# New loads and a computed order for the first 28 slices of a fused attention and gated-FFN kernel

## The chip, the cores and the metric

One core of a Trainium2 chip. The metric is the device time of one execution in microseconds (us). Spans in traces (first to last instruction) are some 2 us shorter than the device times of the same runs.

## The reference, cut to what matters

```python
# x: (B=8, H=8, S=512, D=64), state: (8, 8, 32, 64); all fp32
scores = scale * x @ state^T ; a = softmax(scores) ; xread = a @ state           # 512 rows per batch
scores2 = scale * state @ x^T ; a2 = softmax(scores2) ; sread = a2 @ x           # 32 rows per batch
y = concat([xread, sread], rows).transpose(0, 2, 1, 3).reshape(B * 544, 512)
out = (relu(y @ w_gate) * (y @ w_val)) @ w_out          # d_ff = 1536
```

The kernel folds the state into the gate and value weights (`U = state @ w`), so a batch's gate and value are `U^T @ a^T`. A batch has 12 gate/value slices of 128 columns of d_ff (`gv`), and 12 output pieces (`o`), each of four 512-column matmuls.

## The kernel before

Loads, in the order of issue:

```python
state_dma(nc.sync, 0, 2)                  # state of batches 0 and 1, fp32, hardware queue
x_dma_cast(0, 2)                          # batch 0 of x, cast to bf16 on load, by gpsimd's queue
make_identity(nc, id128)
nc.gpsimd.memset(xa[:, :, :, D:D + 1], 1.0)
for i in range(6):
    for s, d in ws:                       # ws = gate weights, value weights: cast on load
        w_dma(s, d, 256 * i, 256 * i + 256)
    if i == 1:
        x_dma_cast(1)                     # batch 1 behind two weight pairs
x_dma_cast(2); state_dma(nc.gpsimd, 2, B); wo_dma(0, 6); wo_dma(6, NF); x_dma(3, (nc.gpsimd,))
```

The head, up to the 28th gate/value slice, is a written order; what runs before the first slice is called the prelude below. Each engine does its own words from left to right. `spin` is a matmul on zeros for the clock, `xT`/`xo` a transpose of x and its copy out of PSUM, `sc`/`ex`/`nr`/`nx` scores, exp, row sum with reciprocal, scaling, `aT`/`ao` the transpose of the weights of attention and its copy, `c`/`co` (and `u`/`uo`) a fold (state times weights) and its eviction, the copy out of PSUM, to U, `ga`+`gb` one slice, `re` its ReLU on ACT, `mu` its product on VectorE (DVE), `o` an output piece, `sr` the state-read:

```text
spin.7 spin.1 stc.0.2.dve stT.0.2 sto.0.2.0.dve sto.0.2.1.dve xT.0.0 xT.0.1 xo.0.1.dve xo.0.0.act xT.0.3
xo.0.3.dve sc.0.0 xT.0.2 xo.0.2.dve ex.0.0 sc.0.1 nr.0.0 ex.0.1 c.0.0 nx.0.0 ...      # first slice soon after
... (cut)
```

After it a loop does one slice, one output piece and what is hung on that slice:

```python
for b in range(B):
    s, jf = {0: (2, 2), 1: (2, 3), 2: (2, 7), 3: (2, 11)}.get(b, (b - 1, 9))
    if b > 1:
        at(s, jf, sr, b)                  # state-read of batch b at slice jf of round s
```

PSUM: six banks in rotation for everything but the output (`ps_r`), two for the output.

The softmax here doesn't subtract the row's maximum and nothing guards it: scores larger than these inputs give would overflow.

Of the kernel before, what the change touches and what calls it, by code (L numbers as in the profile page):

```python
# [16 lines left out]
def kernel(  # L17
# [35 lines left out]
    ps_r = pool("ps_r", 6, PS)  # L53
    ps_o = pool("ps_o", 1, PS)
# [25 lines left out]
    def bank(name, o=None):  # L80

        if o is None:
            return ps_r.tile([128, 512], FP32, name=name, tag="r")
        return ps_o.tile([128, 512], FP32, name=name, tag=f"o{o}")
# [57 lines left out]
    def x_conv(b, half, eng):  # L142
        if half == 0:
            xb_alloc(b)
            xb[b] = xb[b].rearrange("p (c h d) -> p c h d", c=NC, h=H)
        hs = slice(HK * half, HK * half + HK)
        copy[eng](out=xb[b][:, :, hs].rearrange("p c h d -> p h c d"), in_=xf[b][:, hs])  # L147
# [9 lines left out]
    def x_T(b, j):  # L157

        if j == 0:
            xT_alloc(b)  # L160
        ps = bank("xT_ps").bitcast(BF16)[:, 0:512].rearrange("p (c t) -> p c t", c=NC)
        for c in range(NC):
            if b in cast_on_load:
                for h2 in range(2):
                    nc.tensor.transpose(ps[64 * h2:64 * h2 + 64, c], xb[b][:, c, 2 * j + h2], id128)  # L165
            else:
                nc.tensor.transpose(ps[:, c], xb[b][:, c, 2 * j:2 * j + 2].rearrange("p h d -> p (h d)"), id128)
        held["xT", b, j] = ps
# [5 lines left out]
    def att_sc(b, jp):  # L174
        if jp == 0:
            e_sn[b] = att.tile([128, 2, NC, NJ * Ns], BF16, name="e_sn", tag="e_sn", bufs=4)
            a_sn[b] = att.tile([128, 2, NC, NJ * Ns], BF16, name="a_sn", tag="a_sn")
        t = held["sc", b, jp] = bank("sc_ps")
        ps = t.rearrange("p (r c j n) -> p r c j n", r=2, c=NC, j=2)
        for c in range(NC):  # L180
            for jj in range(2):
                nc.tensor.matmul(ps[:, :, c, jj], xT[b][:, c, 2 * jp + jj], stT[:, b, 2 * jp + jj],  # L182
                                 start=True, stop=True)
# [15 lines left out]
    def att_scale(b, jp):  # L199
        e_v = by_pair(e_sn[b], jp).rearrange("p r (j n) -> p r j n", n=Ns)  # L200
        nc.vector.tensor_tensor(out=by_pair(a_sn[b], jp).rearrange("p r (j n) -> p r j n", n=Ns), in0=e_v,  # L201
                                in1=held["rc", b, jp].to_broadcast([128, 2 * NC, 2, Ns]), op=ALU.mult)
# [9 lines left out]
    def att_T(b, kc):  # L212
        if kc == 0:
            ans_alloc(b)
# [74 lines left out]
    def gv(b, jf, kcs=(0, 1)):  # L289
        if jf == 0 and kcs[0] == 0:  # L290
            hsb[b] = hpool.tile([128, NF, S], BF16, name="h_sb", tag="h_sb")
        if kcs[0] == 0:
            held["gv", b, jf] = [bank("gv_ps"), bank("gv_ps")], hsb[b][:, jf], S
        for w in range(2):
            for kc in kcs:
# [21 lines left out]
    o_n = [0]  # L317

    def o_bank():
        o_n[0] += 1  # L320
        return bank("o_ps", o_n[0] % 2)
# [11 lines left out]
    def fin_x(b, tsub):  # L333
        o_sb = opool.tile([128, d_model], FP32, name="o_sb", tag="o_sb")
        nc.scalar.copy(out=o_sb, in_=held["o", b, tsub])  # L335
# [36 lines left out]
    state_dma(nc.sync, 0, 2)  # L372
    x_dma_cast(0, 2)
# [4 lines left out]
    for i in range(6):  # L378
        for s, d in ws:
            w_dma(s, d, 256 * i, 256 * i + 256)  # L380
        if i == 1:
            x_dma_cast(1)
# [11 lines left out]
    warm_ps = bank("warm_ps", 0)  # L394

    def spin(n):
        for i in range(n):
            nc.tensor.matmul(warm_ps, warm[:, 0:128], warm, start=True, stop=True)
# [80 lines left out]
    for b in range(B):  # L479
        s, jf = {0: (2, 2), 1: (2, 3), 2: (2, 7), 3: (2, 11)}.get(b, (b - 1, 9))  # L480
# [48 lines left out]
```

## Time and profile before

| | before |
|---|---|
| device time, median of 3 | 231.95 us |
| span in the trace | 228.9 us |
| TensorE busy | 219.0 us, 96% |
| first gate/value slice | 14.21 us |
| first output slice | 36.29 us |
| slice 28, start of the loop | 59.21 us |

To read it: an engine at 96% can gain only where it is not busy or where it does nothing useful. The stages are cut at the first of a new kind of work, because the share of a whole span hides which stage is limited by what. The lines are in the prediction.

### The profile page before, as it was taken

The numbers are of one execution on the slowest core, as the hardware profiler recorded it, in microseconds if no ns is written. First come the engines' busy times: TensorE is split into PE (matmuls) and PEld (weight loads), VectorE is DVE, ScalarE is ACT, GpSimd is POOL, SyncE is SP. The second block draws the span as 40 slices with busy tenths as digits, with TensorE's granted clock in tenths as the row PEclk, the third lists the DMA queues.
The fourth block names the chain that finished last, engine by engine and source line by source line (L and its number), as shares of the span: only waits on it lengthen the run. The fifth ranks groups of instructions, "written<-read, shape, count | busy, mean of one in ns | idle before, by whom it ended". The sixth has DMA issues, their size and how long they took to land.

```text
span 228.9 us, 4751 instructions
## 1 busy us (share of the span) xinstructions
PE 219.0 (96%) x1916; PEld 105.1 (46%) x1916; DVE 133.5 (58%) x237; ACT 121.1 (53%) x233; POOL 43.1 (19%) x46
## 2 busy tenths in 40 slices
PE   7589899999998999999999999999999999999994
PEld 3345445454443444344444454444443444666543
DVE  3669878984669646764676568556765344222100
ACT  2469776664775645565555555554655444332221
POOL 8926252341052060006000510000000000000000
PEclk9769999999999999999999999999999999999999
DMA  7999999071715911393139413911311111111132
GB/s 100 174 195 196 214 217 272 21 137 49 223 54 112 279 63 54 79 222 115 53 90 224 146 46 92 140 46 46 94 46 49 46 47 47 49 47 64 73 95 92
DMA packets 36950, 25.21 MB, mean 110 GB/s; under 512 B 17248, under 2 KB 32352, under 8 KB 36928
## 3 DMA queue, kind: packets, MB, share of 16 engines
q1 hardware_dynamic: 25168, 16.78, 27.3%
q0 software_dynamic: 11424, 7.73, 21.5%
q10 hardware_dynamic: 336, 0.39, 0.7%
q8 instruction: 15, 0.25, 0.4%
q14 instruction: 7, 0.06, 0.1%
HBM read 18.35 MB, written 8.91 MB: 119 GB/s over the span
## 4 chain that ended last, share of the span: by engine, by line
PE 85%; DMA 9%; DVE 2%; POOL 1%; issue 1%; ACT 1%; POOLq 0%
PE o_ps L327 37%; PE gv_ps L286 34%; DMA wv_sb<-in_moe_w_val_dram 6%; PE gv_ps L304 5%; PE up L261 4%; DMA wg_sb<-in_moe_w_gate_dram 3%; PE sc_ps L182 1%; PE sr_ps L234 1%; DMA out_dram<-o_sb 1%; DVE a_sn L201 1%; PE upc L261 1%; POOL xb L112 1%; PE xT_ps L165 0%; PE srT_ps L247 0%; PE stT_ps L132 0%
## 5 line engine op out<-in xcount | busy, mean ns | idle before, releaser
L286 PE MATMUL gv_ps<-ans,U 128*128 128x512 bf16 x384 | 97.1, 381 | 1.1 <-DVE U L271 1.0
L327 PE MATMUL o_ps<-wo_sb,h_sb 128*128 128x512 bf16 x372 | 94.8, 379 | 0.0
L315 DVE TENSOR_TENSOR h_sb<-gv_ps,g_sb 128x512 bf16<-128x512 f32 x96 | 64.7, 688 | 42.6 <-ACT g_sb L311 38.3
L311 ACT ACTIVATE g_sb<-gv_ps 128x512 bf16<-128x512 f32 (+1 forms) x108 | 62.1, 578 | 45.7 <-PE gv_ps L286 34.8
L286 PEld LDWEIGHTS <-U 128*128 128x128 bf16 x384 | 35.3, 98 | 42.8 <-issue 5.7
L327 PEld LDWEIGHTS <-h_sb 128*128 128x128 bf16 x372 | 36.0, 98 | 41.1 <-issue 0.9
L335 ACT COPY o_sb<-o_ps 128x512 f32<-128x512 f32 x31 | 18.1, 585 | 21.5 <-PE o_ps L327 21.5
L271 DVE CAST U<-up 128x512 bf16<-128x512 f32 x35 | 22.5, 685 | 6.1 <-PE up L261 6.1
L271 ACT CAST U<-up 128x512 bf16<-128x512 f32 x37 | 19.9, 594 | 10.5 <-PE up L261 10.4
L147 POOL CAST xb<-xf 128x1024 bf16<-128x1024 f32 x10 | 10.6, 1089 | 68.9 <-DMA xf<-in_x_dram 48.8
L195 DVE TENSOR_REDUCE cs<-e_sn 128x16 f32<-128x512 bf16 x16 | 10.9, 683 | 9.2 <-ACT e_sn L189 9.2
L226 POOL COPY xa<-xb 128x2048 bf16<-128x2048 bf16 x8 | 15.0, 1896 | 5.7 <-issue 4.2
L315 DVE TENSOR_TENSOR hs_sb<-gv_ps,g_sb 128x256 bf16<-128x256 f32 x12 | 5.1, 425 | 15.3 <-PE gv_ps L304 10.5
L189 ACT ACTIVATE e_sn<-sc_ps 128x512 bf16<-128x512 f32 x16 | 9.6, 601 | 7.4 <-PE sc_ps L182 7.4
L201 DVE TENSOR_TENSOR a_sn<-e_sn,rc 128x512 bf16<-128x512 bf16 x16 | 12.4, 775 | 0.5
L261 PEld LDWEIGHTS <-stT 64*32 64x32 bf16 x480 | 5.3, 92 | 11.2 <-issue 10.3
L281 ACT CAST U<-upc 128x512 bf16<-128x512 f32 x14 | 7.6, 592 | 3.5 <-PE upc L261 3.4
L182 PEld LDWEIGHTS <-xT 128*128 128x128 bf16 x128 | 5.8, 100 | 4.0 <-DVE xT L171 0.7
L261 PE MATMUL up<-wg_sb,stT 64*32 64x512 bf16 x144 | 7.4, 386 | 0.0
L182 PE MATMUL sc_ps<-stT,xT 128*128 128x64 bf16 x128 | 6.7, 196 | 0.5 <-DVE xT L171 0.5
L304 PE MATMUL gv_ps<-br,wg_sb 128*128 128x256 bf16 x48 | 7.2, 273 | 0.0
L304 PE MATMUL gv_ps<-br,wv_sb 128*128 128x256 bf16 x48 | 7.2, 273 | 0.0
(54 smaller groups left out, 115.1 us busy)
## 6 DMA issues: line engine op xcount, KB each, us to landing
out_dram<-o_sb SPq DMA_DIRECT2D x31, 256.0 KB, 2.4
xf<-in_x_dram SPq DMA_DIRECT2D x4, 1024.0 KB, 6.0
wg_sb<-in_moe_w_gate_dram POOLq DMA_DIRECT2D x6, 256.0 KB, 11.3
wv_sb<-in_moe_w_val_dram POOLq DMA_DIRECT2D x6, 256.0 KB, 10.8
wo_sb<-in_moe_w_out_dram POOLq DMA_DIRECT2D x2, 768.0 KB, 15.1
xb<-in_x_dram POOLq DMA_DIRECT2D x2, 512.0 KB, 11.1
xf<-in_x_dram POOLq DMA_DIRECT2D x1, 1024.0 KB, 18.8
xb<-in_x_dram POOLq DMA_DIRECT2D x2, 256.0 KB, 4.7
```

What stands on the lines that cost most here:

```text
L182: nc.tensor.matmul(ps[:, :, c, jj], xT[b][:, c, 2 * jp + jj], stT[:, b, 2 * jp + jj], start=True, stop=True)
L195: nc.vector.reduce_sum(out=cs, in_=e_v, axis=AX.X)
L201: nc.vector.tensor_tensor(out=by_pair(a_sn[b], jp).rearrange("p r (j n) -> p r j n", n=Ns), in0=e_v, in1=held["rc", b, jp].to_broadcast([1 ...
L226: nc.gpsimd.tensor_copy(out=v.rearrange("p c h d -> p h c d"), in_=xb[b].rearrange("p c h d -> p h c d"))
L261: nc.tensor.matmul(dst[parity][32 * j:32 * j + 32], stT[r:r + 64, b, j, 32 * parity:32 * parity + 32], wsb[r:r + 64, j, lo:lo + n], start= ...
L271: copy[eng](out=U[b][:, w, kc, lo:lo + 512], in_=held["u", b, w, lo][kc])
L286: nc.tensor.matmul(ps[w], U[b][:, w, kc, f0:f0 + 128], ANS[b][:, kc].rearrange("p c t -> p (c t)"), start=(kc == 0), stop=(kc == NK - 1))
L304: nc.tensor.matmul(ps[w][:, 0:nt], wsb[:, j, f0:f0 + 128], br[:, j].rearrange("p b n -> p (b n)"), start=(j == 0), stop=(j == NJ - 1))
L311: nc.scalar.activation(out=g_sb[:, 0:n], in_=ps[0][:, 0:n], func=AF.Relu)
L315: nc.vector.tensor_tensor(out=dst, in0=ps[1][:, 0:n], in1=held["g", b, jf][:, 0:n], op=ALU.mult)
L327: nc.tensor.matmul(held["o", b, tsub], src[:, jf, tsub * 128:(tsub + 1) * 128], wo_sb[:, jf], start=(jf == 0), stop=(jf == NF - 1))
L335: nc.scalar.copy(out=o_sb, in_=held["o", b, tsub])
```

## The change

Intent: load batch 0 faster as plain fp32 on both hardware queues, have batch 1 early enough to do its attention before the first slice, keep the clock up with short spins in the waits, and take the order of the head and its PSUM banks from a computed schedule.

```diff
-    state_dma(nc.sync, 0, 2)
-    x_dma_cast(0, 2)
+    xf[0] = xin.tile([128, H, NC, D], FP32, name="xf", tag="xf")
+    for half in range(2):
+        for eng, h in ((nc.sync, HK * half), (nc.scalar, HK * half + 2)):
+            eng.dma_start(out=xf[0][:, h:h + 2], in_=x[0, h:h + 2].rearrange("h (p c) d -> p h c d", c=NC))
+        if half == 0:
+            state_dma(nc.sync, 0, 2)
+    x_dma_cast(1, 2)
...
-        if i == 1:
-            x_dma_cast(1)
...
+    given, turn = [], {"r": 0, "o": 0}      # bank(): the banks that a word names with @, else in turn
...
-    spin.7 spin.1 stc.0.2.dve stT.0.2 sto.0.2.0.dve sto.0.2.1.dve xT.0.0 xT.0.1 ...
+    stc.0.2.dve spin.4 spin.3.128 stT.0.2@0 sto.0.2.0.act xc.0.0.dve sto.0.2.1.act spin.8.128 xT.0.1@1 xT.0.0@2
+    xo.0.1.dve xo.0.0.act xc.0.1.dve spin.14.128 sc.0.0@3 xT.0.3@4 ex.0.0 xT.0.2@5 xo.0.3.act nr.0.0 xo.0.2.act
+    spin.22.128 sc.0.1@0 nx.0.0 xT.1.0@1 ... spin.11.128 gv.0.1@12 ...      (the rest of the head is cut)
...
-        s, jf = {0: (2, 2), 1: (2, 3), 2: (2, 7), 3: (2, 11)}.get(b, (b - 1, 9))
+        s, jf = {0: (2, 2), 1: (2, 3), 2: (2, 8), 3: (2, 11)}.get(b, (b - 1, 9))
```

`xc` is VectorE's conversion of half of batch 0. The last line: the state-read of batch 2 moves one slice later.

More of the change, by code (lines that the diff above doesn't have):

```diff
@@ L52 @@
     PS = bass.MemoryType.PSUM
-    ps_r = pool("ps_r", 6, PS)
-    ps_o = pool("ps_o", 1, PS)
+    psum = pool("psum", 1, PS)
     NK = 2
@@ L78, with bank @@
     copy = {"act": nc.scalar.copy, "dve": nc.vector.tensor_copy, "pool": nc.gpsimd.tensor_copy}
-    def bank(name, o=None):
-        if o is None:
-            return ps_r.tile([128, 512], FP32, name=name, tag="r")
-        return ps_o.tile([128, 512], FP32, name=name, tag=f"o{o}")
+    given, turn = [], {"r": 0, "o": 0}
+    def bank(name, kind="r"):
+        if given:
+            n = given.pop(0)
+        else:
+            n = turn["r"] % 6 if kind == "r" else 6 + turn["o"] % 2
+            turn[kind] += 1
+        return psum.tile([128, 512], FP32, name=name, tag=f"b{n}")
     held = {}
@@ L142, in x_conv @@
     def x_conv(b, half, eng):
-        if half == 0:
+        if b not in xb:
             xb_alloc(b)
@@ L157, in x_T @@
     def x_T(b, j):
-        if j == 0:
+        if b not in xT:
             xT_alloc(b)
@@ L174, in att_sc @@
     def att_sc(b, jp):
-        if jp == 0:
+        if b not in e_sn:
             e_sn[b] = att.tile([128, 2, NC, NJ * Ns], BF16, name="e_sn", tag="e_sn", bufs=4)
@@ L197, in att_sum, with att_scale @@
         nc.vector.reciprocal(out=rc, in_=cs)
-    def att_scale(b, jp):
+    def att_scale(b, jp, eng="dve"):
         e_v = by_pair(e_sn[b], jp).rearrange("p r (j n) -> p r j n", n=Ns)
-        nc.vector.tensor_tensor(out=by_pair(a_sn[b], jp).rearrange("p r (j n) -> p r j n", n=Ns), in0=e_v,
+        {"dve": nc.vector, "pool": nc.gpsimd}[eng].tensor_tensor(out=by_pair(a_sn[b], jp).rearrange("p r (j n) -> p r j n", n=Ns), in0=e_v,
                                 in1=held["rc", b, jp].to_broadcast([128, 2 * NC, 2, Ns]), op=ALU.mult)
@@ L212, in att_T @@
     def att_T(b, kc):
-        if kc == 0:
+        if b not in ANS:
             ans_alloc(b)
@@ L287, in gv_mm, with gv @@
                          start=(kc == 0), stop=(kc == NK - 1))
-    def gv(b, jf, kcs=(0, 1)):
-        if jf == 0 and kcs[0] == 0:
+    def gv(b, jf):
+        if b not in hsb:
             hsb[b] = hpool.tile([128, NF, S], BF16, name="h_sb", tag="h_sb")
-        if kcs[0] == 0:
-            held["gv", b, jf] = [bank("gv_ps"), bank("gv_ps")], hsb[b][:, jf], S
+        held["gv", b, jf] = [bank("gv_ps"), bank("gv_ps")], hsb[b][:, jf], S
         for w in range(2):
-            for kc in kcs:
+            for kc in range(NK):
                 gv_mm(held["gv", b, jf][0], b, jf, w, kc)
@@ L315, in mult @@
         nc.vector.tensor_tensor(out=dst, in0=ps[1][:, 0:n], in1=held["g", b, jf][:, 0:n], op=ALU.mult)
-    o_n = [0]
     def o_bank():
-        o_n[0] += 1
-        return bank("o_ps", o_n[0] % 2)
+        return bank("o_ps", "o")
     def out_mms(src, b, tsub, jfs):
@@ L331, in out_rows, with fin_x @@
         return out[b * SP: b * SP + S].rearrange("(p q) m -> q p m", q=NC)[tsub]
-    def fin_x(b, tsub):
+    def fin_x(b, tsub, eng="act"):
         o_sb = opool.tile([128, d_model], FP32, name="o_sb", tag="o_sb")
-        nc.scalar.copy(out=o_sb, in_=held["o", b, tsub])
+        copy[eng](out=o_sb, in_=held["o", b, tsub])
         nc.sync.dma_start(out=out_rows(b, tsub), in_=o_sb)
@@ L392, in x_next, with spin @@
         x_trans_dma(b)
-    warm_ps = bank("warm_ps", 0)
-    def spin(n):
+    warm_ps = psum.tile([128, 512], FP32, name="warm_ps", tag="b7")
+    def spin(n, cols=512):
         for i in range(n):
-            nc.tensor.matmul(warm_ps, warm[:, 0:128], warm, start=True, stop=True)
-    steps = {"spin": spin, "stc": state_conv, "stT": state_T, "sto": state_out, "xT": x_T, "xo": x_out,
+            nc.tensor.matmul(warm_ps[:, 0:cols], warm[:, 0:128], warm[:, 0:cols], start=True, stop=True)
+    steps = {"spin": spin, "stc": state_conv, "stT": state_T, "sto": state_out, "xc": x_conv, "xT": x_T, "xo": x_out,
@@ L403 @@
              "sc": att_sc, "ex": att_exp, "nr": att_sum, "nx": att_scale, "aT": att_T, "ao": att_out,
-             "c": c_unit, "co": c_out, "u": u_unit, "uo": u_out, "ga": lambda b, jf: gv(b, jf, (0,)),
-             "gb": lambda b, jf: gv(b, jf, (1,)), "re": relu, "mu": mult, "o": out_part,
-             "of": lambda b, t, eng: fin_x(b, t), "xn": x_next, "xp": x_pad, "sr": lambda b: (sr_mm(b), sr_norm(b))}
+             "c": c_unit, "co": c_out, "u": u_unit, "uo": u_out, "gv": gv, "re": relu, "mu": mult, "o": out_part,
@@ L407 @@
+             "of": fin_x, "xn": x_next, "xp": x_pad, "sr": sr_mm, "sn": sr_norm}
     program = """
-    spin.7 spin.1 stc.0.2.dve stT.0.2 sto.0.2.0.dve sto.0.2.1.dve xT.0.0 xT.0.1 xo.0.1.dve xo.0.0.act xT.0.3
-    xo.0.3.dve sc.0.0 xT.0.2 xo.0.2.dve ex.0.0 sc.0.1 nr.0.0 ex.0.1 c.0.0 nx.0.0 co.0.0.0.act co.0.0.1.act
-    nr.0.1 c.1.0 co.1.0.0.act nx.0.1 aT.0.0 aT.0.1 ao.0.0.act c.0.1 co.1.0.1.dve c.1.1 ao.0.1.dve co.0.1.1.dve ga.0.0
-    gb.0.0 co.0.1.0.act co.1.1.1.dve ga.0.2 co.1.1.0.act gb.0.2 re.0.0 re.0.2 ga.0.3 gb.0.3 mu.0.0 ga.0.1 mu.0.2
@@ L412 @@
-    re.0.3 gb.0.1 re.0.1 xT.1.0 xT.1.1 xo.1.0.act mu.0.3 xT.1.2 xo.1.2.act xT.1.3 mu.0.1 xo.1.1.dve stc.2.8.pool xp.0 xp.1
-    xo.1.3.dve c.0.2 co.0.2.0.act sc.1.0 co.0.2.1.dve c.1.2 co.1.2.0.dve sc.1.1 ex.1.0 co.1.2.1.act ga.0.5 gb.0.5
-    nr.1.0 ex.1.1 re.0.5 ga.0.4 gb.0.4 c.0.3 nx.1.0 re.0.4 mu.0.5 co.0.3.0.act co.0.3.1.act mu.0.4 c.1.3
-    co.1.3.1.act c.0.4 nr.1.1 co.0.4.0.dve co.1.3.0.act ga.0.6 gb.0.6 ga.0.7 gb.0.7 co.0.4.1.act nx.1.1
-    re.0.6 ga.0.9 re.0.7 gb.0.9 aT.1.0 aT.1.1 mu.0.6 ao.1.0.act ga.0.8 mu.0.7 re.0.9 ao.1.1.dve gb.0.8 ga.1.0 gb.1.0 re.0.8 mu.0.9
@@ L417 @@
-    ga.1.1 re.1.0 gb.1.1 mu.0.8 mu.1.0 ga.1.6 re.1.1 mu.1.1 gb.1.6 ga.1.3 gb.1.3 ga.1.2 re.1.6 gb.1.2 re.1.3 mu.1.6
-    re.1.2 mu.1.3 stT.2.4 ga.1.5 gb.1.5 ga.1.7 mu.1.2 sto.2.4.1.act sto.2.4.0.act re.1.5 gb.1.7 ga.1.4 gb.1.4
-    re.1.7 mu.1.5 re.1.4 o.0.0 c.0.5 xT.2.0 co.0.5.0.act mu.1.7 mu.1.4 xT.2.1 xT.2.3 xT.2.2 co.0.5.1.dve xo.2.1.dve
-    c.1.5 xo.2.0.act xo.2.2.dve ga.0.11 xo.2.3.act gb.0.11 ga.0.10 co.1.5.1.dve re.0.11 co.1.5.0.dve gb.0.10
-    mu.0.11 ga.1.10 sc.2.0 gb.1.10 re.0.10 ex.2.0 mu.0.10 nr.2.0 re.1.10 ga.1.11 gb.1.11 sc.2.1 re.1.11 o.0.1
@@ L422 @@
-    mu.1.10 o.0.2 ex.2.1 mu.1.11 c.1.4 u.2.0.0 u.2.1.0 co.1.4.1.act o.0.3 nx.2.0 co.1.4.0.dve uo.2.0.0.1.dve
-    uo.2.1.0.0.act uo.2.0.0.0.act nr.2.1 uo.2.1.0.1.act ga.1.8 gb.1.8 nx.2.1 ga.1.9 gb.1.9 xn.3 re.1.8 of.0.0.act mu.1.8
-    sr.0 sr.1 xp.2 xp.3 o.0.4 re.1.9 mu.1.9 aT.2.0 aT.2.1 o.0.5 ao.2.0.dve ao.2.1.act of.0.1.act ga.2.0 ga.2.3 ga.2.1 gb.2.0 gb.2.1 re.2.0 mu.2.0
-    re.2.1 o.0.6 ga.2.2 gb.2.3 mu.2.1 re.2.3 mu.2.3 gb.2.2 re.2.2 o.0.7 o.0.8 u.2.0.512 mu.2.2
-    u.2.1.1024 of.0.2.act uo.2.0.512.1.dve uo.2.0.512.0.act u.2.1.512 o.0.9 uo.2.1.512.0.dve u.2.0.1024
@@ L427 @@
-    uo.2.1.1024.1.act uo.2.1.512.1.act uo.2.1.1024.0.dve uo.2.0.1024.0.dve uo.2.0.1024.1.act
+    stc.0.2.dve spin.4 spin.3.128 stT.0.2@0 sto.0.2.0.act xc.0.0.dve sto.0.2.1.act spin.8.128 xT.0.1@1 xT.0.0@2
+    xo.0.1.dve xo.0.0.act xc.0.1.dve spin.14.128 sc.0.0@3 xT.0.3@4 ex.0.0 xT.0.2@5 xo.0.3.act nr.0.0 xo.0.2.act
+    spin.22.128 sc.0.1@0 nx.0.0 xT.1.0@1 ex.0.1 xT.1.1@2 xo.1.0.dve xo.1.1.act nr.0.1 spin.5.128 xT.1.2@3 xT.1.3@4
+    sc.1.0@5 xo.1.3.act xo.1.2.dve ex.1.0 nx.0.1 spin.8.128 sc.1.1@0 ex.1.1 nr.1.0 spin.5.128 aT.0.0@1 aT.0.1@2
@@ new lines @@
+    ao.0.1.act spin.2.128 c.0.0@43 ao.0.0.dve c.1.0@50 co.0.0.1.dve co.0.0.0.act co.1.0.0.act nr.1.1 spin.11.128
+    gv.0.1@12 co.1.0.1.act nx.1.0 re.0.1 gv.0.0@43 nx.1.1 re.0.0 c.0.1@50 mu.0.1 aT.1.1@1 co.0.1.0.act aT.1.0@4
+    co.0.1.1.dve ao.1.1.act c.1.1@25 ao.1.0.dve co.1.1.0.act gv.0.3@01 mu.0.0 co.1.1.1.act re.0.3 c.0.2@42 gv.1.1@35
+    co.0.2.0.act mu.0.3 co.0.2.1.act c.1.2@04 re.1.1 gv.0.5@12 co.1.2.1.dve co.1.2.0.act mu.1.1 re.0.5 gv.1.3@34
+    mu.0.5 re.1.3 gv.0.2@01 mu.1.3 re.0.2 c.0.3@53 mu.0.2 gv.1.5@24 co.0.3.0.act co.0.3.1.dve re.1.5 gv.1.0@01 mu.1.5
@@ new lines @@
+    re.1.0 gv.1.2@52 mu.1.0 re.1.2 c.0.4@34 mu.1.2 gv.0.6@01 co.0.4.1.act co.0.4.0.act c.1.3@52 re.0.6 gv.0.7@43
+    co.1.3.0.dve co.1.3.1.act mu.0.6 re.0.7 gv.0.4@05 mu.0.7 re.0.4 gv.0.8@24 mu.0.4 re.0.8 gv.1.6@13 stc.2.8.pool
+    xp.0 xp.1 xn.3 mu.0.8 re.1.6 xT.2.2@0 xT.2.3@5 mu.1.6 xo.2.2.act xT.2.1@2 xT.2.0@4 stT.2.4@1 xo.2.3.act xo.2.1.dve
+    c.0.5@30 xo.2.0.dve sto.2.4.0.act gv.1.4@25 co.0.5.0.dve co.0.5.1.act sto.2.4.1.dve gv.1.7@43 re.1.4 re.1.7 mu.1.4
+    gv.0.9@01 mu.1.7 re.0.9 gv.0.10@24 mu.0.9 re.0.10 sc.2.1@5 gv.0.11@30 mu.0.10 ex.2.1 re.0.11 nr.2.1 sc.2.0@1
@@ new lines @@
+    o.0.0@6 ex.2.0 mu.0.11 c.1.5@25 c.1.4@43 nx.2.1 co.1.5.1.act u.2.0.1024@10 o.0.1 uo.2.0.1024.1.dve co.1.4.1.act
+    co.1.4.0.act nr.2.0 o.0.2 co.1.5.0.dve gv.1.8@53 of.0.0.act nx.2.0 re.1.8 o.0.3@7 uo.2.0.1024.0.dve mu.1.8
+    gv.1.10@04 re.1.10 o.0.4 mu.1.10 aT.2.0@2 o.0.5 ao.2.0.dve u.2.1.0@51 of.0.1.act u.2.0.512@30 u.2.1.1024@42
+    uo.2.1.0.1.act o.0.6@6 uo.2.1.1024.0.dve uo.2.0.512.1.act uo.2.0.512.0.act aT.2.1@1 o.0.7 uo.2.1.0.0.act
+    ao.2.1.dve uo.2.1.1024.1.act sr.0@4 u.2.1.512@03 sn.0 u.2.0.0@15 uo.2.1.512.0.dve o.0.8 uo.2.0.0.0.act
@@ L428 @@
+    uo.2.1.512.1.dve uo.2.0.0.1.act gv.1.11@24 of.0.2.act re.1.11 gv.2.3@01 mu.1.11 re.2.3 gv.2.2@53 mu.2.3 re.2.2
+    gv.2.1@24 mu.2.2 re.2.1 gv.2.0@01 mu.2.1 re.2.0 gv.1.9@53 mu.2.0 re.1.9 o.0.9@7 mu.1.9 sr.1@2 sn.1 xp.2 xp.3
     """
     for word in program.split():
+        word, _, banks = word.partition("@")
+        given.extend(int(n) for n in banks)
         name, *args = word.split(".")
         steps[name](*(int(v) if v.isdigit() else v for v in args))
+        assert not given
     units = {}
```

## The prediction

> **What bounds the kernel now.** I read the page first (busy shares, then the 40 slices), then the chain that ended last in order of time, then busy time by stage with the stages cut where the chain changes character, then the timeline of the first 60 us engine by engine.
>
> ```profile
> PE 219.0 (96%) x1916; PEld 105.1 (46%) x1916; DVE 133.5 (58%) x237; ACT 121.1 (53%) x233; POOL 43.1 (19%) x46
> PE   7589899999998999999999999999999999999994
> PEclk9769999999999999999999999999999999999999
> DMA  7999999071715911393139413911311111111132
> ```
>
> TensorE is busy 96% of the span; the only slices below 8 are the first two and the last. So only the head can give anything: no change here removes useful matmuls. The granted clock dips in slices 2 and 3.
>
> ```profile
> 5.01 6.73 DMA wg_sb<-in_moe_w_gate_dram
> 12.03 12.73 DMA wv_sb<-in_moe_w_val_dram
> 25.10 2.70 PE gv_ps L286 x12
> 36.46 0.86 PE o_ps L327 x4
> 44.77 0.34 PE upc L261 x16
> 59.28 0.97 PE gv_ps L286 x4
> ```
>
> These are pieces of the chain (start, length, what). Until 24.75 us it hangs on two weight loads; from 25.10 it is TensorE all the way. The 28th gate/value slice starts at 59.2 us; after it the loop that the change leaves alone begins. So everything is decided by when TensorE reaches that point.
>
> ```profile
> 0.00:14.21 14.21, 9.53 (x132) 4.84 (x132) 7.80 (x19) 5.70 (x10) 11.49 (x21) 0.80 1.11 148
> 14.21:25.03 10.82, 9.90 (x160) 4.99 (x153) 9.24 (x17) 9.33 (x18) 5.17 (x6) 0.95 1.45 197
> 25.03:36.29 11.26, 11.26 (x68) 5.33 (x61) 8.74 (x14) 8.36 (x19) 4.50 (x3) 1.00 1.29 218
> 36.29:59.21 22.92, 22.92 (x297) 10.81 (x295) 17.38 (x33) 14.38 (x27) 5.75 (x4) 1.00 0.41 109
> ```
>
> Columns: window, length, busy PE, PEld, DVE, ACT, POOL, granted clock, DMA share, GB/s. 14.21 us is the first gate/value slice, 36.29 the first output slice. DVE and ACT are over 85% busy from 14.21 to 25.03, and about 76% in the next stage. The weight queue moves 197 GB/s (bf16 written, so about 390 GB/s read) without a break.
>
> How much of the head is lost? Useful TensorE work by spacing in the chain and timeline: a gate/value or output slice 0.86, a 256-column weight fold (upc) 0.34, a 512-column one 0.21, four transposes 0.22 to 0.25, a score half 0.23, a state-read 0.64. The head has 28 + 10 slices (32.8), 12 folds (4.1), 6 wide folds (1.3), 12 transposes of x (3.0), 6 of the weights of attention (1.3), 6 score halves (1.4), two of the state (0.7), two state-reads (1.3): 45.9 us. It takes 59.2, so 13.3 are lost: 14.2 − 3.6 useful (four folds, batch 0's transposes and scores) = 10.6 before the first slice, about 2.4 from there to 25 (0.5 of it half clock, 0.8 the wait for a value-weight piece), next to nothing later.
>
> [...] cast loads sustain about 390 GB/s of reading, and the plain fp32 megabytes of x on the sync queue took 3.0 to 4.1 us, 256 to 350 GB/s. [...] The state's cast here, 128x256, took 293 ns; [...] half clock is recorded from 8.4 to 15.25 us, after a window in which TensorE was about half busy. The first 8 warm-up matmuls are 0.43 apart, half speed, although the windows print 1.00 there.
>
> **The change part by part.** (a) *Loads.* Before: state landed at 3.03, batch 0's halves at 5.36 and 7.38, the first two weight pairs by 13.1, batch 1 at 16.8, the last value piece at 27.5. After: hardware packets can start at 1.86 as the state's did. Two quarters of x are 32 packets of 1 KB per engine; at the 42 ns per packet per engine of the cast queue that is 1.35 us, so the first half lands near 3.8. The state now stands behind a quarter of x on its ring [...] so I put it at 5.0 (4.0 to 6.4) instead of 3.03. The second half lands near 7.3. Batch 1 lands near 9, the first weight pair 1 to 2 us later than before, pieces 2 to 5 some 1 to 2 earlier, because the whole sum of bytes is the same and begins about 1 us sooner.
>
> (b) *Prelude.* DVE converts the state before it converts x, so the chain starts at the state's landing S: convert 0.29, first half 0.69, transposes and copies 0.8, then exp, sum and reciprocal (0.60 + 0.68 + 0.25) for the first heads while the second half is converted and copied by ACT (2 x 0.59); second score half at S+4.5, exp 0.60, sums 0.94, scale 0.70, with two copies of batch 1 (0.42 each) between; transposes at S+7.6, their copies to S+8.9, fold and its eviction 0.69: first slice at S+9.65. With S = 5.0 it is 14.65; I take 14.8 for some spins at half clock. So it is **not earlier than the 14.21 of before**. What is bought is that batch 1's transposes, scores and most of its softmax are done by then.
>
> (c) *First slice to first output slice.* TensorE has 20 slices, 8 folds, transposes, scores: 17.3 + 2.7 + 2.3 = 22.3. ACT has 19 ReLUs, 12 fold evictions, 5 others: 19 x 0.60 + 12 x 0.59 + 3.1 = 21.6. DVE has 19 products, 5 folds, 2 sums, 2 scales, 4 copies: 19 x 0.69 + 5 x 0.69 + 5.1 = 21.6. Back to back they go faster (five ACT evictions in 2.72, two DVE ones in 1.28), so about 20. [...] Walking the order by hand with the banks it names, TensorE waits for a bank in some ten places, 0.1 to 0.6 each, the most just after the first slice (fold, attention transposes and slice 3 all wait for evictions). I get 23.4, a loss of about 1.1.
>
> (d) *Output slices to slice 28.* 8 + 10 slices 15.5, folds 2.0, rest 1.8: 19.3. The output slices need no product, DVE and ACT catch up, and the same walk finds almost no wait.
>
> Sum: 14.8 + 23.4 + 19.3 = 57.5 against 59.2: **1.7 us saved**, and 231.95 − 1.7 = 230.2. The spins cost nothing by themselves: they fill waits. Named banks and the split of the gate/value slice into one step add no instruction.
>
> **Rivals.** *State early.* If the ring gives the state its turn at once (S near 3.4), the first slice comes at 13.1 and, with evictions at the back-to-back rate, the end of the head at 55: about 227.5. For it: a 128 KB state load took only 0.84 us of packets; against: three queues are active. *Spins in the way.* If the clock stays half through the prelude, 22 spins of 128 columns are 2.3 us instead of 1.2 and lie in front of the score matmul; the first slice comes at 16.5, and 231.9 or a little more results. For it: only seven spins at the start, then an idle wait for the state, about what left the clock at half before. *Weights too late.* The third weight piece is needed some 3.3 us after the first slice, about 18, and should land at 17 to 18; a lag gives 0.5 us. The first value piece (11.6 to 12.4) is needed at about S+8, which is a tie. *Evictions worse than walked.* DVE and ACT at 90% instead of 93% use cost about 0.8.
>
> **Range and chances.** S moves the time one for one by −1.6 to +1.4, evictions by ±1, the clock by up to +1.5. Eight in ten: 227.6 to 232.6. Over 2% faster means under 227.3, which needs the early state and full-rate evictions together: 0.17. Over 2% slower means above 236.6, and nothing costs 4.7 us unless a load queues badly: 0.03. Within 2%: 0.80.
>
> **What would show it.** Right: the state's cast starts at 4 to 6 us, a half of x converts in 0.69, the first gate/value slice starts at 14 to 15.5, DVE and ACT are over 85% busy from it to the first output slice, that one lies near 38, slice 28 starts near 57.5, and the span after it is unchanged near 169.8. Wrong: a first slice before 13.5 (then the time is below 228.5), a clock still half beyond 12 us, or TensorE waiting for a weight DMA.

## The result, and the profile after

Ratios here are the mean time of one kernel's fast runs over that of the other's fast runs of the same rounds, so not quite the ratio of the medians quoted.

| | before | after |
|---|---|---|
| device time, median of 4 | 231.93 us | 229.88 us (229.66 to 230.72) |
| ratio, 95% interval | | 0.9919 (0.9891 to 0.9948) |
| span in the trace | 228.9 | 227.6 |
| state converted by VectorE from | 3.05 | 5.41 |
| first gate/value slice | 14.21 | 16.28 |
| first output slice | 36.29 | 39.49 |
| slice 28 | 59.21 | 58.72 |
| from slice 28 to the end | 169.7 | 168.9 |

The page of the changed kernel, the same three slice rows as before:

```profile
PE   3999999999999999999999999999999999999993
PEclk9999999999999999999999999999999999999999
DMA  7999999254217911591139213611311111112132
```

TensorE now looks full from the second slice on, and the clock looks full throughout. Both are misleading here. Much of the early busy time is spins, and the clock row prints full speed before the first record of a clock change, here and in the kernel before (windows of it print 1.00 from 1.60 to 5.01 us, where the wide spins are 0.43 us apart, and the four matmuls of an output slice, of 512 columns too, take 0.86 at full clock later); the first record of this trace is a change to full clock at 8.87 us. The spacing of spins shows the half clock before it: the 8 spins of 128 columns from 6.47 us take 1.03 here, as in the control of the spins experiment, and 0.71 where the clock became full at 6.71.

The stages, by the columns explained in the prediction:

```profile
0.00:16.28 16.28, 12.59 (x207) 10.23 (x207) 8.83 (x19) 8.48 (x18) 11.89 (x21) 1.00 1.17 198
16.28:39.49 23.21, 22.86 (x266) 10.63 (x269) 19.51 (x35) 19.93 (x39) 8.93 (x8) 1.00 1.28 224
39.49:58.72 19.23, 18.75 (x227) 8.63 (x227) 14.43 (x25) 12.12 (x23) 4.38 (x3) 1.00 0.45 126
58.72:227.60 168.88, 164.07 (x1266) 79.15 (x1276) 88.77 (x157) 82.83 (x161) 17.53 (x13) 1.00 0.31 88
```

The two middle stages last 23.21 and 19.23 us. The first lasts 16.28, two more than before, and the last is 0.8 shorter although the loop's work is the same. (TensorE's count in the last row is a little short: some matmul records are missing.)

Pieces of the chain (the work that ended last, followed back through what released it) up to the first slices, by start, length and what:

```profile
1.26 4.13 DMA st_f<-in_state_dram
5.41 0.45 DVE st_b L129
5.90 0.63 PE stT_ps L136 x4
6.54 0.97 PE warm_ps L401 x8
7.50 0.85 PE xT_ps L171 x8
8.36 1.09 PE warm_ps L401 x14
9.44 0.23 PE sc_ps L186 x8
10.12 1.23 PE warm_ps L401 x22
...
16.92 0.25 DVE rc L201
17.17 0.20 DVE a_sn L205
...
18.31 0.60 DVE h_sb L318
18.91 0.60 DVE U L285
19.51 0.33 DVE ans L225
19.84 0.61 DVE h_sb L318
20.45 0.07 issue
20.52 0.41 PE upc L265 x16
```

The chain hangs on the state's load to 5.39 us, then on TensorE's spins and transposes, then (14.4 to 20.45) on VectorE, which does batch 1's softmax, evictions and the first products one after the other. From 20.52 it is TensorE. Before, the chain hung on weight loads until 24.75; that wait is gone, and a slower beginning has taken its place.

Landings from the trace's records: state 5.39, batch 0 at 4.38 and 7.93 (first and second half), batch 1 at 7.79 and 9.14, first weight pair 10.47 and 11.85, last value piece 26.09. The first packet of the cast load of batch 1 moved at 4.82, although the load was issued from 1.24; in the kernel before, with nothing but the state on the hardware queues, the first cast packet moved at 2.86, of a load issued from 1.24 too.

So the time fell about as much as forecast, but not where. The head gained 0.5 us of the 1.7 forecast, and the loop, forecast as unchanged, gained 0.8 by the end of the span (1.2 by the position of the products, see the first experiment). The experiments ask three things: what the one digit does, what holds the first slice, and what holds the stage behind it.

### The profile page after: what moved, and what is told of

Its sections match the earlier page's. It is cut to its first block, busy times and chain, and to the rows that moved or that the text cites. A ratio compares the mean times of both kernels' runs of the same rounds, so it can differ in the third digit from the quotient of the medians.

```text
span 227.6 us, 4847 instructions
## 1 busy us (share of the span) xinstructions
PE 218.3 (96%) x1945; PEld 108.6 (48%) x1974; DVE 131.5 (58%) x233; ACT 123.4 (54%) x239; POOL 42.7 (19%) x45
## 4 chain that ended last, share of the span: by engine, by line
PE 90%; DVE 3%; DMA 3%; ACT 1%; issue 1%; SPq 0%
PE o_ps L327 38%; PE gv_ps L290 35%; PE gv_ps L307 5%; PE up L265 4%; DMA st_f<-in_state_dram 2%; PE warm_ps L401 2%; PE sc_ps L186 2%; PE sr_ps L238 1%; PE upc L265 1%; PE xT_ps L169 1%; DMA out_dram<-o_sb 1%; PE stT_ps L136 1%; DVE cs L199 1%; PE xT_ps L171 1%; ACT U L285 1%
## 5 line engine op out<-in xcount | busy, mean ns | idle before, releaser
L290 PE MATMUL gv_ps<-ans,U 128*128 128x512 bf16 x366 | 94.8, 380 | 0.7
L327 PE MATMUL o_ps<-wo_sb,h_sb 128*128 128x512 bf16 x361 | 93.6, 379 | 1.1 <-issue 0.5
L318 DVE TENSOR_TENSOR h_sb<-gv_ps,g_sb 128x512 bf16<-128x512 f32 x96 | 65.1, 687 | 39.5 <-ACT g_sb L314 38.5
L205 DVE TENSOR_TENSOR a_sn<-e_sn,rc 128x512 bf16<-128x512 bf16 x16 | 11.7, 737 | 0.4
L285 ACT CAST U<-upc 128x512 bf16<-128x512 f32 x17 | 9.4, 600 | 1.3 <-PE upc L265 1.3
L401 PE MATMUL warm_ps<-warm 128*128 128x128 bf16 (+1 forms) x82 | 8.5, 259 | 1.2 <-DVE warm L370 1.2
L265 PEld LDWEIGHTS <-stT 64*32 64x32 bf16 x480 | 4.5, 89 | 9.9 <-issue 9.3
L401 PEld LDWEIGHTS <-warm 128*128 128x128 bf16 x82 | 5.9, 111 | 2.8 <-issue 1.5
L265 PE MATMUL up<-wv_sb,stT 64*32 64x512 bf16 x144 | 7.2, 377 | 0.0
```

Source lines behind the costliest of these rows:

```text
L205: {"dve": nc.vector, "pool": nc.gpsimd}[eng].tensor_tensor(out=by_pair(a_sn[b], jp).rearrange("p r (j n) -> p r j n", n=Ns), in0=e_v, in1= ...
L265: nc.tensor.matmul(dst[parity][32 * j:32 * j + 32], stT[r:r + 64, b, j, 32 * parity:32 * parity + 32], wsb[r:r + 64, j, lo:lo + n], start= ...
L290: nc.tensor.matmul(ps[w], U[b][:, w, kc, f0:f0 + 128], ANS[b][:, kc].rearrange("p c t -> p (c t)"), start=(kc == 0), stop=(kc == NK - 1))
L318: nc.vector.tensor_tensor(out=dst, in0=ps[1][:, 0:n], in1=held["g", b, jf][:, 0:n], op=ALU.mult)
L327: nc.tensor.matmul(held["o", b, tsub], src[:, jf, tsub * 128:(tsub + 1) * 128], wo_sb[:, jf], start=(jf == 0), stop=(jf == NF - 1))
L401: nc.tensor.matmul(warm_ps[:, 0:cols], warm[:, 0:128], warm[:, 0:cols], start=True, stop=True)
```

## The experiments

All twelve ran with five rounds beside the kernel before on the same chip; the medians are of six runs, four for e5 and five for e7, and of eleven of the kernel before. The record marks every result correct, that of e12 too, although its edit makes it wrong. Three sets on three chips; set 1 holds no run of the changed kernel itself:

| set | run | median us | before, median us | ratio (95%) |
|---|---|---|---|---|
| 1 | digit alone (e1) | 230.35 | 231.24 | 0.9960 (0.9936 to 0.9985) |
| 1 | all but the digit (e2) | 231.24 | 231.24 | 1.0005 (0.9979 to 1.0030) |
| 1 | state's load first (e3) | 229.21 | 231.24 | 0.9919 (0.9897 to 0.9940) |
| 1 | no later spins (e4) | 230.55 | 231.24 | 0.9973 (0.9951 to 0.9995) |
| 2 | the changed kernel again (e8) | 230.30 | 231.86 | 0.9929 (0.9905 to 0.9953) |
| 2 | more spins at the start (e5) | 229.08 | 231.86 | 0.9878 (0.9851 to 0.9906) |
| 2 | new loads, old order (e6) | 233.22 | 231.86 | 1.0050 (1.0024 to 1.0076) |
| 2 | old loads, new order (e7) | 236.36 | 231.86 | 1.0206 (1.0178 to 1.0234) |
| 3 | combined (e9) | 228.29 | 231.31 | 0.9875 (0.9848 to 0.9903) |
| 3 | digit alone again (e10) | 230.54 | 231.31 | 0.9965 (0.9939 to 0.9990) |
| 3 | all but the digit again (e11) | 231.41 | 231.31 | 1.0001 (0.9980 to 1.0022) |
| 3 | half of the ReLU (e12) | 230.24 | 231.31 | 0.9948 (0.9926 to 0.9970) |

### The digit, and everything but the digit

e1 is the kernel before with the digit, e2 the changed kernel without it; e10 and e11 are the same two again in one set.

```diff
-        s, jf = {0: (2, 2), 1: (2, 3), 2: (2, 7), 3: (2, 11)}.get(b, (b - 1, 9))
+        s, jf = {0: (2, 2), 1: (2, 3), 2: (2, 8), 3: (2, 11)}.get(b, (b - 1, 9))
```

> The kernel before with one word changed: the state-read of batch 2 one slice later (slice 8 instead of 7 of its round), as the changed kernel has it. Theory A (the 1.2 us that the changed kernel gains after slice 28 come from this word: in the kernel before the state-read frees a buffer at 67.96 us, GpSimd's 1.9 us copy starts, and VectorE's scaling of the scores beside it takes 1.85 instead of 0.69): 1.2 us faster than before, about 230.7, no scaling over 1 us in the loop's first round, TensorE's 1 us wait at 71 gone. Theory B (the gain comes from the new order of the head, which leaves GpSimd and VectorE with less to catch up): within 0.3 us of before.

> The changed kernel with that word put back (state-read of batch 2 at slice 7). Theory A: about 1.2 us slower than the changed kernel, 231.1, and the 1.85 us scaling is back. Theory B: the changed kernel's 229.9 within 0.3.

> The one-word version (the kernel before with the state-read of batch 2 a slice later) again, in one set with the next run so that the two parts of the change stand against the same runs of before. If the word carries most of the gain: ratio 0.994 to 0.996.

> The other part alone: new loads, order and spins with the state-read where it was. If the word carries most of the gain: ratio 0.997 to 1.000. If the head carries it: below 0.995.

Measured: the digit alone gives 0.9960 and 0.9965, 0.8 to 0.9 us. The whole rest of the change, loads, order, spins and banks, gives 1.0005 and 1.0001: nothing that these runs resolve. That is theory A; the forecast 1.2 us would be 0.9948, which lies inside both intervals. In the traces it is 1.2: the 37th product stands 0.45 us earlier than before in e2 and 1.60 in the changed kernel. It is 1.2 in either order of the head: from the 29th product to the last are 133.26 us before and 132.08 in e1, 133.49 in e2 and 132.32 in the changed kernel.

The collision, in three traces. First the kernel before, VectorE's scaling of batch 3's scores, GpSimd's copy for the state-read of batch 4, and TensorE's matmuls after it:

```profile
68.55 1.85 DVE L201 TENSOR_TENSOR a_sn<-e_sn,rc 128x512 bf16<-128x512 bf16 x1
67.96 1.90 POOL L226 COPY xa<-xb 128x2048 bf16<-128x2048 bf16 x1 [1.30 <-PE sr_ps L234]
69.46 0.59 PE L286 MATMUL gv_ps<-ans,U 128*128 128x512 bf16 x2
71.05 0.59 PE L286 MATMUL gv_ps<-ans,U 128*128 128x512 bf16 x2 [0.99 <-DVE U L271]
```

Then e1, with the digit:

```profile
68.36 0.69 DVE L201 TENSOR_TENSOR a_sn<-e_sn,rc 128x512 bf16<-128x512 bf16 x1
69.61 1.90 POOL L226 COPY xa<-xb 128x2048 bf16<-128x2048 bf16 x1 [3.14 <-PE sr_ps L234]
```

And e2, the changed kernel without it:

```profile
68.10 1.85 DVE L205 TENSOR_TENSOR a_sn<-e_sn,rc 128x512 bf16<-128x512 bf16 x1
67.51 1.90 POOL L230 COPY xa<-xb 128x2048 bf16<-128x2048 bf16 x1 [4.64 <-PE sr_ps L238]
```

The state-read's end releases GpSimd's copy (the releaser in brackets). Where the copy begins just before the scaling, the scaling takes 1.85 instead of 0.69 us and ends 0.54 us after the copy does (68.55 + 1.85 = 70.40; 67.96 + 1.90 = 69.86). The fold's evictions behind it on VectorE come late and TensorE waits 0.99. One slice later the copy begins after the scaling and nothing waits. Why the scaling takes longer beside the copy is not shown; its time fits a wait for the copy's end. Scalings of over 0.8 us stand beside this copy in before, e2 and e11 (1.85 us each) and beside GpSimd's conversion of x in before (0.87, at 44.21 us) and in the changed kernel (1.53, at 40.66): each of these five began 0.05 to 0.71 us after the GpSimd instruction did, and each ended 0.54 us after that instruction's end. Not every such meeting costs time: the one at 40.66 us is in the changed kernel, yet from the first output slice to the 29th product it needs 20.50 us, as e5 and e9 do, which have no such scaling.

The two parts do not add up exactly: 0.996 times 1.000 against 0.9919 and 0.9929 for both. Each interval is a quarter of a per cent either way, so whether the head gains some 0.3% once the digit is in stays open.

### What holds the first slice: the order of two loads

```diff
+    state_dma(nc.sync, 0, 2)
     for half in range(2):
         for eng, h in ((nc.sync, HK * half), (nc.scalar, HK * half + 2)):
             eng.dma_start(out=xf[0][:, h:h + 2], in_=x[0, h:h + 2].rearrange("h (p c) d -> p h c d", c=NC))
-        if half == 0:
-            state_dma(nc.sync, 0, 2)
```

> The changed kernel with the state's load ahead of the first quarter of x on the sync queue, nothing else. Theory A (the prelude hangs on the state's landing, 5.39 us, because VectorE converts it before x): the state lands near 3.0, the first half of x near 4.6, the first gate/value slice comes 0.8 to 1.5 us earlier than 16.28, and so does the end: 228.4 to 229.1. Theory B (the prelude hangs on the second half of x or on batch 1, which landed at 7.93 and 9.1, or on spins): under 0.4 us gained.

Both theories missed in part. The state was converted from 4.48 (not 3.0: beside loads of x it took 3.72 us from issue to landing, and 2.29 without them), and the first half of x landed later for it (5.64 at VectorE). The first slice came at 16.30, as in the changed kernel. In this trace the clock became full only at 10.07, and its chain shows what that took: the state's transposes begin 0.73 us earlier than in the changed kernel (5.17 against 5.90), and the 14 spins, scores and transposes of the chain after them last 2.68 us instead of 1.77. The runs together give 0.9919, as the changed kernel had it on another chip. No gain is shown: the 0.73 us gained before that stretch were lost in it (0.91 us longer; its 14 spins, at half clock, took 1.70 against 1.29).

### What holds the first slice: the spins and the clock

e4 leaves the 75 spins of 128 columns behind the state's transposes out; e5 makes the ones at the start longer.

```diff
# e4_no_later_spins: from the program up to the first slice
-    ... sto.0.2.1.act spin.8.128 xT.0.1@1 ... xc.0.1.dve spin.14.128 sc.0.0@3 ... spin.22.128 sc.0.1@0 ...
+    ... sto.0.2.1.act xT.0.1@1 ... xc.0.1.dve sc.0.0@3 ... sc.0.1@0 ...
# e5_spins_to_state
-    stc.0.2.dve spin.4 spin.3.128 stT.0.2@0
+    stc.0.2.dve spin.9 spin.3.128 stT.0.2@0
```

> The changed kernel without the 75 spins of 128 columns behind the state's transposes; the seven at the start stay. Theory A (they stand in front of useful matmuls at half clock, three groups of them are pieces of the chain, 0.97 + 1.09 + 1.23 us): the score matmuls come sooner and the first slice 0.5 to 1 us earlier as long as the clock is not worse. Theory B (without them TensorE is too idle for the full clock, as in the kernel before, whose half clock lasted to 15.25 us): half clock to 12 us or beyond, the first slice no earlier than 16.3 and the time 230 to 231.

> The changed kernel itself, as the control on the chip of this set. With the word alone worth 0.9 us on the last chip and the state-first version at 229.2 there: 229.3 to 230.2, about 1 us below the one-word version's ratio of 0.996.

> The changed kernel with nine instead of four wide spins at the very start, so that TensorE is busy until the state lands near 5.4 us. Theory A (the prelude loses time to the half clock, which lasted to 8.87 us because TensorE idles from 3.4 to 5.9): full clock by 5 to 7 us, the spins of 128 columns and the transposes behind it at 0.056 apart, first gate/value slice 0.6 to 1.0 us earlier than in the control. Theory B (the chain of conversions, exp and sums holds the first slice, spins only fill): within 0.3 us of the control.

Without the later spins the clock stays half until 14.79 us, the first slice comes at 16.89 and the ratio is 0.9973, against 0.9919 and 0.9929 with them on other chips (and 0.9919 of e3 in the same set): theory B. The spins do stand in the chain, and they are still worth having: without them TensorE was at half clock up to 14.79 of the 16.89 us of the prelude.

With more spins at the start the clock is full from 6.71 us, the first slice comes at 15.65 and the ratio is 0.9878 against 0.9929 of the control in the same set, 1.2 us: theory A. TensorE in e5, then in the control, whose clock became full at 11.86:

```profile
1.19 4.34 PE L401 MATMUL warm_ps<-warm 128*128 128x512 bf16 x12 [1.19 <-DVE warm L370]
6.49 0.71 PE L401 MATMUL warm_ps<-warm 128*128 128x128 bf16 x8
7.48 0.94 PE L401 MATMUL warm_ps<-warm 128*128 128x128 bf16 x14
9.49 1.39 PE L401 MATMUL warm_ps<-warm 128*128 128x128 bf16 x22
15.65 1.89 PE L290 MATMUL gv_ps<-ans,U 128*128 128x512 bf16 x8
```

```profile
1.19 2.21 PE L401 MATMUL warm_ps<-warm 128*128 128x512 bf16 x7 [1.19 <-DVE warm L370]
6.47 1.03 PE L401 MATMUL warm_ps<-warm 128*128 128x128 bf16 x8
8.15 1.70 PE L401 MATMUL warm_ps<-warm 128*128 128x128 bf16 x14
10.93 1.84 PE L401 MATMUL warm_ps<-warm 128*128 128x128 bf16 x22
17.54 1.89 PE L290 MATMUL gv_ps<-ans,U 128*128 128x512 bf16 x8
```

The control's 14 spins take 1.70 where e5's take 0.94. The five traces whose prelude is that of the changed kernel, with the first record of full clock and the start of the first slice:

| trace | full clock from | first slice |
|---|---|---|
| changed kernel | 8.87 | 16.28 |
| all but the digit (e2) | 8.95 | 16.32 |
| half of the ReLU (e12) | 9.43 | 16.62 |
| all but the digit again (e11) | 10.49 | 16.89 |
| changed kernel again (e8) | 11.86 | 17.54 |

From the first row to the last the clock comes 3.0 us later and the slice 1.26, so each us of half clock costs about 0.4 here. The second half of x also landed later in the last two rows (8.64 and 8.96 against 7.82 to 8.02), but that is not what held e8: its half was converted by 9.74, and TensorE reached the transposes of it at 10.09. The prelude is the same in all five: where the clock turns differs from run to run. The traced run of e8 was the slowest of its six (229.56 to 230.90), that of the changed kernel the fastest of its four; for the untraced runs the turn is not known. e5, whose traced clock was up early, spread less (228.82 to 229.25).

What goes with the difference stands in the traces. The changes of the clock lie whole multiples of 3.41 us apart (5.01, 8.42 and 15.25 in the kernel before; 8.87 and 227.32, 64 times 3.41, in the changed kernel). Cut each trace into windows of 3.41 us that end at them: in the eleven traces for which the record of full clock is quoted in this document (before, the changed kernel, e2 to e6, e8, e9, e11 and e12), half clock became full after windows with 2.97 us or more of TensorE busy, and after none with 2.54 or less (busy times are modelled, and the clock before the first record is taken as half, as the spacing of spins shows). That sorts these eleven traces; why the clock changes is not shown. Where the windows begin differs: the one from 5.46 to 8.87 in the changed kernel held 2.97 us, the one from 5.04 to 8.45 in e8 held 2.54, since more of the idle wait up to 5.9 fell into it. With e5's longer spins no window has more than 0.4 us of that wait.

### Loads and order apart

e6 is the kernel before (with the digit) with the new loads and VectorE's two conversions put into the old order; e7 is the changed kernel with the old loads and without the conversions.

```diff
# e6_new_loads_old_order
-    ... sto.0.2.1.dve xT.0.0 xT.0.1 xo.0.1.dve xo.0.0.act xT.0.3 ...
+    ... sto.0.2.1.dve xc.0.0.dve xT.0.0 xT.0.1 xo.0.1.dve xo.0.0.act xc.0.1.dve xT.0.3 ...
# e7_old_loads_new_order
-    ... sto.0.2.0.act xc.0.0.dve sto.0.2.1.act spin.8.128 ... xo.0.0.act xc.0.1.dve spin.14.128 ...
+    ... sto.0.2.0.act sto.0.2.1.act spin.8.128 ... xo.0.0.act spin.14.128 ...
```

> The kernel before with the new loads (batch 0 in fp32 by both hardware queues and converted by VectorE, batch 1 ahead of the weights) and the state-read at slice 8, but its own order of work. Theory A (the loads only pay with the order that uses batch 1 early): the first weight pair lands 1.5 to 2 us later and is what the old order asks for first, so the first slice comes 1 to 2.5 us later than 14.1 and the time is 1 to 2 us above the one-word version, 231.5 to 232.5. Theory B (the loads are the gain): at or below the one-word version.

> The changed kernel's order with the loads of before (state first, batch 0 cast on load, batch 1 behind two weight pairs), no conversion by VectorE. Batch 1 lands at 16.8 us and its transposes stand in TensorE's order ahead of the first weight fold, so the first slice cannot come before about 19.5 to 20.5: 3 to 4 us slower than the control, 233 to 234. If it is within 1 us of the control the place of batch 1's load is of no account.

The new loads in the old order give 1.0050, 2 us worse than the digit alone in the other sets: the first slice comes at 17.37 with the clock at half until 19.51. The old loads in the new order give 1.0206, more than expected: TensorE stands 6.29 us before batch 1's transposes and the first slice comes at 22.80.

```profile
16.34 1.06 PE L169 MATMUL xT_ps<-id,xb 128*64 128x128 bf16 x16 [6.29 <-DMA xb<-in_x_dram]
```

Each half of the head's change is a loss alone; together they come out even. The order needs batch 1 early, and the new loads that bring it early also bring the state at 5.39 instead of 3.03 us and the first weight pair 1.4 to 1.7 later.

### What holds the stage behind the first slice

The changed kernel with a wrong result: for batches 0 and 1 ACT takes the ReLU of 256 of 512 columns and VectorE reads those twice.

```diff
-        nc.scalar.activation(out=g_sb[:, 0:n], in_=ps[0][:, 0:n], func=AF.Relu)
+        m = 256 if b < 2 else n
+        nc.scalar.activation(out=g_sb[:, 0:m], in_=ps[0][:, 0:m], func=AF.Relu)
...      # the product, for b < 2: in1 = g_sb[:, 0:256] broadcast to [128, 2, 256]
```

> The changed kernel with a wrong result on purpose: for batches 0 and 1 the ReLU takes half of the columns and VectorE reads that half twice, so each of those evictions costs ACT about 0.21 us less and VectorE the same. Theory A (between the first gate/value slice and the first output slice TensorE waits for banks that ACT and VectorE empty): that stage shrinks from 23.2 us by 0.5 to 1.2. Theory B (TensorE's own work, some 22.3 us, and its waits for VectorE hold it): by less than 0.3.

Busy time from 16 to 39.5 us, the changed kernel, then this one:

```profile
16.00:39.50 23.50, 23.15 (x272) 10.92 (x275) 19.80 (x35) 20.23 (x40) 8.93 (x8) 1.00 1.28 223
```

```profile
16.00:39.50 23.50, 23.50 (x279) 10.93 (x272) 19.85 (x35) 16.42 (x41) 8.95 (x8) 1.00 1.28 223
```

ACT's busy time (the sixth column, counts in brackets aside) falls from 20.23 to 16.42, and from the first slice to the first output slice it is 39.84 − 16.62 = 23.22 us, as in the changed kernel (23.21). Theory B: ACT's time does not hold this stage. It is the same 23.22 in e5 and in e9. The chain shown above names VectorE up to 20.45 and TensorE afterwards; no run here made VectorE faster, so its part is read from the chain and not tested.

### Combined

The changed kernel with the state's load first, seven wide spins instead of four at the start, and batch 1's load behind the identity on GpSimd.

```diff
-    x_dma_cast(1, 2)
     nc.scalar.activation(out=tiny, ...)
     make_identity(nc, id128)
     nc.gpsimd.memset(xa[:, :, :, D:D + 1], 1.0)
+    x_dma_cast(1, 2)
...      # state_dma(nc.sync, 0, 2) first, as in the state-first run
-    stc.0.2.dve spin.4 spin.3.128 stT.0.2@0
+    stc.0.2.dve spin.7 spin.3.128 stT.0.2@0
```

> The changed kernel with the three things that the earlier runs point to: the state's load first on the sync queue, seven wide spins at the start so that TensorE is busy until the state lands, and batch 1's cast load issued by GpSimd after the identity and the ones column (about 1 us later), so that it takes less from batch 0's second half. Theory A (with the clock full, the first slice hangs on the landing of the second half of x, 8.19 us in the version with more spins): the second half lands by 7.3, the first slice comes at 14.5 to 15.2 instead of 15.65, and the ratio to before is 0.983 to 0.986. Theory B (a load gained is a load lost[...]): 0.987 to 0.989, as with the spins alone.

In the trace it is theory A: second half of x at 6.62 instead of 7.93, clock full from 4.23, first slice at 14.95, span 226.2, the shortest of all. In time it is 228.29 us and 0.9875 (0.9848 to 0.9903), which is in theory B's range, beside 0.9878 of the spins alone, and 3.0 us below the kernel before by the medians; one of its six runs was at 229.78. Both beat the kernel before, and the ratios of the changed kernel by about half a per cent (e9 on a chip where the changed kernel did not run); which of the two is the better one these runs do not decide. GpSimd's reordering moved the issue by 0.23 us only (1.24 to 1.47), and batch 1's loads took 6.9 us from issue to landing (median of two), 6.8 in the changed kernel.

## Why the prediction was right or wrong

Predicted 230.2, measured 229.88: the time was right within 0.3 us, and by luck. Two of its steps were wrong and nearly cancelled: the head came 1.2 us later than forecast, and the loop, forecast as unchanged, was 0.8 shorter.

- **(a) Loads: right within 0.6 us.** State 5.39 against 5.0, first half 4.38 against 3.8, second 7.93 against 7.3, batch 1 at 9.14 against 9, first weight pair 1.4 to 1.7 later against 1 to 2, last value piece 1.4 earlier against 1 to 2. The 5.0 for the state was the author's estimate and supposed that its packets would move beside those of the cast load. They did not: the state's moved from 3.61 to 4.77, the cast load's first at 4.82.
- **(b) Prelude: the step that failed.** "I take 14.8 for some spins at half clock" was 16.28, and 16.3 to 17.5 in the other traces of the same prelude. Of the 1.5 us in the profiled run 0.4 is the state's landing. The mis-sized term is the half clock: I gave it 0.15 us, and against e5's trace (full from 6.71, slice at 15.65) it cost 0.6 in this trace and 1.9 in e8's. Some 0.6 us is left even with e5's clock: its state landed at 5.42, so S+9.65 would be 15.07. There the chain hangs on the second half of x, which landed at 8.19 and not at 7.3. (The terms listed for S+9.65 come to S+9.59.) The text had the half clock as the rival *Spins in the way*, with 16.5 for the first slice, which is what came, and the right reason for it (seven spins, then an idle wait for the state). It should have been the main line, since the trace of before showed half clock from 8.42 us, after 3.41 us with TensorE busy for 1.87. The more-spins run confirms it by 1.2 us in the medians. The rival was wrong in one respect: the cure is more spins and not fewer.
- **(c) First slice to first output slice: 23.4 against 23.2, right in size, partly wrong in reason.** The walk put TensorE's waits down to banks that ACT and VectorE empty. Taking 3.8 us off ACT did not shorten the stage; VectorE's part was not tested.
- **(d) Output slices to slice 28: 19.3 against 19.23, right.** So the sum missed only through (b): 57.5 predicted, 58.72 measured, 0.5 us saved and not 1.7.
- **"The span after it is unchanged near 169.8": wrong, 168.9.** The working lists what the change moves and passes over one digit, the state-read of batch 2. It carries 0.8 to 0.9 us in time in two sets, and the rest of the change, without it, nothing that shows. The sign was there to be read: the chain of before has a 1.85 us scaling among sixteen whose median is 0.69, in the loop's first round, and behind it stands the only wait of TensorE's matmuls for VectorE in the loop, 0.99 us.
- **Rivals.** *State early* did not occur. *Weights too late* did not: no matmul of the new trace waits for a weight load. *Evictions worse than walked* did not.
- **Signs.** The state's cast in 4 to 6 and the conversion of a half in 0.67 to 0.68 (against 0.69, the author's estimate) were as written, and VectorE and ACT at 84 and 86% nearly so (over 85). The first slice in 14 to 15.5, the first output slice near 38 (39.49), slice 28 near 57.5 (58.72) and the unchanged loop were not, and the clock still half at 8.87 (11.86 in another trace) was near the sign I gave for a wrong prediction.

## What to carry to other kernels

When a large change moves the time by what was forecast, check that it moved where it was forecast; run the parts alone, the one-digit ones too. Here 0.9 us came from keeping one GpSimd copy of 1.90 us out of the way of one VectorE instruction (1.85 us beside it, 0.69 without), and a reworked head came out even, or nearly, with an early idle wait of 2.51 to 2.65 us after which TensorE stayed at half clock until 8.87 to 11.86. Filling that wait with dummy matmuls up to the moment that the data lands was worth 1.2 us, more than the new loads and order showed without it.

## What the traces show of the loads and the clock

- A cast load on gpsimd's queue started late beside loads on the hardware queues: issued from 1.24 us in both kernels, its first packet moved at 2.86 with only the state beside it and at 4.82 with batch 0 on both hardware queues. Why is not shown. With the loads of before in the new order (e7) TensorE's wait for the cast load of batch 0 ended at 5.47, in the kernel before at 5.41, so the new order alone did not delay it.
- In eleven traces half clock became full after windows of 3.41 us with 2.97 us or more of TensorE busy, and after none with 2.54 or less. TensorE busy for 2.2 us and then idle until 5.9 left half clock until 8.87 to 11.86 in five traces; busy until 5.5 gave full clock at 6.71. In the kernel before the clock halved at 8.42 after a window with 1.87 us busy; in e9 it stayed full after one with 2.24 (4.23 to 7.64: 14 spins from 7.11 took 0.94).
- The clock row of the profile of before prints 9 in its first slice, and its windows 1.00, before the first clock record at 5.01 us. The spacing of the first wide spins, 0.43 us, shows half clock there.
